# One core, spectral filter beside a shift-mixing MLP: the second group's statistics and transposes among the first group's products, and step one's pairs, unscalings and maxima in other places

## The chip, the core and the metric

The kernel runs on one core of a Trainium2 chip. The core has TensorE (matmuls and transposes by matmul), VectorE, ScalarE, GpSimd and SyncE, which here issues every DMA. Each engine works off its own instructions in the order in which the program lists them, and waits on semaphores for the others. In the profile TensorE is PE (and PEld for its weight loads), VectorE is DVE, ScalarE ACT, GpSimd POOL and SyncE SP. The metric is the device time of one execution in microseconds; the median of several runs counts.

## What is computed

`x` has 2048 tokens of 448 values. Two branches start from it and are summed with it:

```python
def _A_ref(x, w_r, w_i):                       # spectral filter
    X = rfft2(x); X = X * (w_r + 1j * w_i)
    return irfft2(X, (S, D))

def _B_ref(x, w1, w2, w3, w4):
    h = gelu(layernorm(x) @ w1)
    # the four quarters of h are shifted by +1, -1, +2, -2 tokens
    x1 = x + concat([g0, g1, g2, g3]) @ w2
    return x1 + gelu(layernorm(x1) @ w3) @ w4

xn = layernorm(x)
return x + _A_ref(xn, A_w_r, A_w_i) + _B_ref(xn, B_w1, B_w2, B_w3, B_w4)
```

w1 and w2 are 448 x 448, w3 is 448 x 1792, w4 1792 x 448; the filter has 2048 x 225 complex weights.

## The kernel before, in words

**Tiles.** Sixteen blocks of 128 tokens in four groups (`GRP`): group 0 is blocks 14, 15, 0, 1, group 1 is blocks 2 to 5, and so on. Precision comes from pairs of float16 numbers: a value is split into a high half (a copy by ScalarE) and a low half (the remainder, by VectorE, or GpSimd for some weights), and a product of two such values is three matmuls. A scale that keeps a weight in float16's range is worked out on the chip: for w1, ScalarE sums squares (line 252), VectorE adds them up (line 257), a small matmul with ones spreads the sum over the partitions (line 259), and VectorE makes powers of two of it (lines 261 to 266, `powers`). `split_w` (lines 272 to 280) then splits the weight.

**The start.** TensorE has nothing to do until the first loads land; `warm_up` gives it 24 matmuls on zeros. `norm1(g)` takes mean and variance of a group's four blocks (`bn_stats` and `bn_aggr`, lines 303 and 304), a first guess of the inverse root and an applied normalisation (lines 330 and 333, shared by GpSimd, VectorE and ScalarE), and hands back `refine`, ten small GpSimd instructions. `T1(g)` transposes the group, 16 matmuls into four PSUM banks (line 384), and evacuates each bank in a high half (line 388, ScalarE) and a low half (line 389, VectorE). Then come the products with w1 (line 415): 11 matmuls for each of the group's four units, 44 in all. For group 0 they come in two parts: the first two slices of all four units, 24 matmuls, and then the last two slices, 5 for each unit. After the 44, the sum matmul for w2 and group 1's transposes follow. `w1_unit` evacuates a unit by gelu and a split (lines 455 to 459); block transposes on SyncE and the products with w2 (line 474) finish the mixing.

**The MLP.** `ln2` normalises again (statistics, line 303; high half on ScalarE, line 504; low half on VectorE, lines 505 and 507; a block transpose on SyncE, line 509). `mlp` runs over groups of 256 tokens, `G`, and pairs of slices of w3, `fp`: `front` is 22 matmuls with w3 (line 395), a gelu (line 724) and a split into `hf` (lines 726 and 727); `back` is 12 matmuls with w4 (line 806), two fronts behind.

**Step one of the transform** runs beside the MLP's groups 1 and 2. `do_fold` loads two blocks of x, scales them on ScalarE (line 536) and folds them on GpSimd (lines 542 to 545); `step1_in` splits them (lines 552 and 553); `step1` is 12 matmuls for a block (line 562) into one of two banks, evacuated on ScalarE and VectorE into `y` (lines 566 and 567). Pairs of blocks are placed by the table `PACE` behind the last w4 matmul of a given `(G, fp)`. On VectorE beside it are seven unscalings of the residual (line 515, with loads into one buffer of two halves) and eight maxima over the filter's weights (line 270, with loads into another buffer of two halves); both are placed behind a front's split by `EARLY` and `WMAX`. The same two buffers serve `ln2` before. The maxima end in a scale (`w_scale_end`) that the transform's next step needs. After that come the transform's other steps and the rest of the MLP.

**Order.** A planner lists each engine's instructions by a simulated time and by priority, which goes by the order of the text apart from `prio`; `behind(key)` keeps what it encloses behind an instruction noted in `after`, on the same engine only. So a pin on VectorE doesn't hold the load that the pinned instruction needs.

Of the kernel before, what the change touches and what calls it, by code (L numbers as in the profile page):

```python
# [27 lines left out]
FIRST = 2  # L28
WARM = 24
ZPRE = 2.0 ** -7  # L30
# [94 lines left out]
def body(tc, nc, x, wf, w1, w2, w3, w4, c_g, c_n, c_small, out):  # L125
# [128 lines left out]
    def powers(m, n, key, tag="acc", spare=0):  # L254

        t = pc.tile([128, 2], F32, name=f"pt{key}")
        V.tensor_reduce(out=t[:, 0:1], in_=m[:, :n], axis=AX.X, op=ALU.add)
        pm = bank(tag, f"pm{key}") if isinstance(tag, str) else tag
        i = T.matmul(pm[:, 0:1], ones, t[:, 0:1], start=True, stop=True)
        after["p" + key] = (i.ins,)  # L260
        V.tensor_scalar(out=t[:, 1:2], in0=pm[:, 0:1], scalar1=2.0 ** -58, scalar2=None, op0=ALU.max)
# [3 lines left out]
        V.tensor_scalar(out=e[:, 1:2], in0=e[:, 0:1], scalar1=-1, scalar2=185 - spare << 23, op0=ALU.mult, op1=ALU.add)  # L265
        V.tensor_scalar(out=e[:, 2:3], in0=e[:, 0:1], scalar1=1, scalar2=69 + spare << 23, op0=ALU.mult, op1=ALU.add)
        return e.bitcast(F32)[:, 1:2], e.bitcast(F32)[:, 2:3]
# [4 lines left out]
    def split_w(hi, lo, src, s, low=None):  # L272
        if low is P:
            P.tensor_scalar(out=src, in0=src, scalar1=s, scalar2=0.0, op0=ALU.mult, op1=ALU.add)
# [3 lines left out]
        i = A.activation(out=hi, in_=src, func=AF.Copy, scale=s)  # L278
        j = V.scalar_tensor_tensor(out=lo, in0=src, scalar=s, in1=hi, op0=ALU.mult, op1=ALU.subtract)
        return i.ins, j.ins  # L280
# [16 lines left out]

    def stats(src, key, mv=None):
        if mv is None:
            mv = pc.tile([128, 4, 2], F32, tag="mv", bufs=3, name=f"mv{key}")  # L300
        for i, s in enumerate(src):
            st = pc.tile([128, 6], F32, tag="st", bufs=4, name=f"st{key}_{i}")
            V.bn_stats(out=st, in_=s)
            V.bn_aggr(out=mv[:, i, :], in_=st)
        return mv
# [4 lines left out]

    def norm1(g, apply):

        bs = GRP[g]
        n, b0 = len(bs), bs[0]
        mv = pc.tile([128, 4, 2], F32, name=f"mva{b0}")
        stats([xb(b) for b in bs], f"a{b0}", mv)
        a = pc.tile([128, 2 * n], F32, name=f"va{b0}")
# [58 lines left out]

    def transpose_split(srcs, dst, key, ts=range(4), at=0, tags=("tr",) * 4):
        c = slice(128 * at, 128 * at + 128 * len(srcs))
        for t in ts:
            pt = bank(tags[t], f"pt{key}{t}")  # L380
            w = 128 if t < 3 else 64
            with behind("T", key) if ("T", key) in after else contextlib.nullcontext():
                for i, s in enumerate(srcs):
                    m = T.transpose(pt[:w, 128 * i:128 * i + 128], s[:, 128 * t:128 * t + w], ident)
# [3 lines left out]
            i = A.activation(out=dst[:w, t, c], in_=pt, func=AF.Copy)  # L388
            j = V.tensor_tensor(out=lo, in0=pt, in1=dst[:w, t, c], op=ALU.subtract)  # L389
            after[key, t] = after[key] = i.ins, j.ins  # L390
# [86 lines left out]

    def ln2(bs, engines):

# [21 lines left out]
        for i in range(n):  # L501
            b, h, x_ = b0 + i, y[i // 2][:, i % 2], o[i // 2][:, i % 2]
            k = r[:, i:i + 1]
            u = A.activation(out=h[:, 0:D], in_=x_, func=AF.Copy, scale=k)
# [51 lines left out]
    def step1(b):  # L556
        t = xh_buf[b % 4]
        pm = bank("sp", f"ps1_{b}")
        for q in range(4):
            for n, (xi, ri) in enumerate(PASS):  # L560
                o = xi * 452 + 113 * q
                T.matmul(pm[:, 128 * q:128 * q + 128], t[:, o:o + 128], cR[ri][:, 128 * (q % 2):128 * (q % 2) + 128],  # L562
                         start=n == 0, stop=n == 2)
# [3 lines left out]
        V.tensor_tensor(out=y[1], in0=src, in1=y[0], op=ALU.subtract)  # L567

    sc = pc.tile([128, 4], F32, name="sc")

    def w_scale():
        wm = pc.tile([128, 8], F32, name="wm")
        t = stage("wl", 8 * DF, 1)
        for c in range(8):
            h = t[:, 4 * DF * (c % 2):4 * DF * (c % 2) + 4 * DF]
            SY.dma_start(h, wf.rearrange("c (p r) n -> (c p) (r n)", r=8)[:, 4 * DF * c:4 * DF * (c + 1)])
            with behind("f", *WMAX[c]):
                absmax(wm[:, c:c + 1], h)
        return wm

    def w_scale_end(wm):
        t = pc.tile([128, 4], F32, name="wt")
# [262 lines left out]

    def T1(g, ts=range(4)):
        if g not in xTs:
            xTs[g] = p1.tile([128, 7, 512], F16, tag="xT", bufs=2, name=f"xT{g}")
        transpose_split([xb(b) for b in GRP[g]], xTs[g], f"a{g}", ts,
                        tags=("mm", "mm", "tr", "tr") if g == 2 else ("tr", "tr", "acc", "acc"))  # L850

# [135 lines left out]
    for b in range(12, 16):  # L987
        w2_tile(b)
    ln2(range(12, 16), [P, A, P, A])
    close("p1")  # L990
# [8 lines left out]
    for i in range(4):  # L999
        P.memset(xh_buf[i][:, 904:], 0.0)  # L1000
    loads = stage("loads", 1808, 0)
    EARLY = {(1, 0): 1, (1, 1): 2, (1, 3): 3, (1, 5): 4, (1, 6): 5, (2, 1): 6, (2, 2): 7,
             (2, 3): "4", (2, 4): "5", (2, 5): "0"}

    def between(G, fp):
        if (G, fp) in EARLY:
            k, n = EARLY[G, fp], list(EARLY).index((G, fp))
            part = loads[:, 896 * (n % 2):896 * (n % 2) + 896]
            go = w4_sums(int(k), part) if isinstance(k, str) else unscale(k, part)
            with behind("f", G, fp):  # L1010
                go()

    mlp([1, 2], hook=between, ahead=AH, tags=("mm", "tr"))
    for b in range(0, NB, 2):
# [78 lines left out]
```

## Time and profile before

| | us |
|---|---|
| median of three runs | 412.37 |
| lowest and highest of the runs | 412.36, 414.42 |
| the profiled execution, whole | 414.05 |
| its span, first to last instruction | 412.2 |
| TensorE busy in the span | 401.3 |
| VectorE, ScalarE, GpSimd busy | 333.9, 255.8, 100.9 |

The profiled execution's mean granted TensorE clock is 0.996 of full speed. The profile's rows give a start and a duration, the engine, the line, the operation, what it writes and reads, shapes and a count of merged instructions; in square brackets stands how long the engine sat idle before, and whose end released it. Rows that start with a line number are groups: after the bar come busy microseconds and the mean of one in nanoseconds, after the next bar the idle time ahead of them.

### The profile page before, as it was taken

To read this page: it belongs to the slowest core of one execution; us is meant where nothing else is said; L and a number is where in the kernel's file an instruction comes from. 1 tells how busy PE (TensorE), PEld (TensorE's weight loads), DVE (VectorE), ACT (ScalarE), POOL (GpSimd) and SP (SyncE) were. 2 spreads that over 40 slices of the span, in tenths; PEclk is the share of its full clock that TensorE was granted. 3 is DMA by queue.
4 is the path that set the end of the run, shared out by engine and by line. 5 is a ranking of instruction groups with operands and counts; after the bars stand their busy time and mean duration, and the time that the engine had idled before them with its cause. 6 is when DMAs were issued, how large, how long until landed. Compare 5 with 4: busy or idle time off the path is not lost.

```text
span 412.2 us, 8724 instructions
## 1 busy us (share of the span) xinstructions
PE 401.3 (97%) x3389; PEld 298.0 (72%) x3389; DVE 333.9 (81%) x702; ACT 255.8 (62%) x434; POOL 100.9 (24%) x173
## 2 busy tenths in 40 slices
PE   6999999999999999999999999999999999999996
PEld 2655545755658677777787888877777779998995
DVE  5878998999775858987798888956799998966645
ACT  4679789982567857565498888954453453553331
POOL 7688520110035866420011221110000000000000
PEclk9899999999999999999999999999999999999999
DMA  8976985479297557435355556610021012100101
GB/s 272 377 278 128 245 170 146 81 122 198 54 238 208 173 173 233 139 131 143 84 147 152 147 142 161 163 32 14 0 91 68 25 67 82 56 23 0 46 2 45
DMA packets 54596, 52.07 MB, mean 126 GB/s; under 512 B 35678, under 2 KB 48542, under 8 KB 54556
## 3 DMA queue, kind: packets, MB, share of 16 engines
q1 hardware_dynamic: 54556, 51.53, 46.0%
q8 instruction: 26, 0.43, 0.4%
q14 instruction: 14, 0.11, 0.1%
HBM read 38.28 MB, written 3.67 MB: 102 GB/s over the span
## 4 chain that ended last, share of the span: by engine, by line
PE 60%; DMA 2%; issue 1%; DVE 1%; POOL 0%; SPq 0%
PE pw L395 24%; PE acc L806 16%; PE side L776 4%; PE acc L776 3%; PE pu L665 3%; PE pe L686 2%; PE pp L620 2%; PE px L637 2%; PE py L707 2%; DMA wl<-wf 2%; PE ps L562 1%; DVE wm L270 0%; POOL xr L543 0%; POOL f L545 0%; DVE y L567 0%
## 5 line engine op out<-in xcount | busy, mean ns | idle before, releaser
L395 PE MATMUL pw<-x2mem,w3p 128*128 128x256 f16 x1232 | 150.6, 273 | 0.0
L395 PEld LDWEIGHTS <-w3p 128*128 128x128 f16 x1232 | 119.3, 98 | 19.9
L806 PE MATMUL acc<-w4p,hf 128*128 128x448 f16 (+1 forms) x516 | 105.6, 348 | 0.7 <-ACT hf L726 0.7
L806 PEld LDWEIGHTS <-hf 128*128 128x128 f16 x516 | 49.6, 98 | 37.6 <-ACT hf L726 1.0
L724 ACT ACTIVATE pw<-pw,pe 128x512 f32<-128x512 f32 x42 | 27.4, 653 | 29.4 <-PE pw L395 29.4
L727 DVE SCALAR_TENSOR_TENSOR hf<-pw,h,hf 128x512 f16<-128x512 f32 x42 | 31.3, 745 | 12.8 <-ACT hf L726 12.7
L415 PE MATMUL pw<-w1p,xT 128*128 128x448 f16 x176 | 35.5, 356 | 1.1 <-DVE xT L389 0.6
L474 PE MATMUL pw<-w2p,h 128*128 128x448 f16 x176 | 35.6, 353 | 0.9 <-DMA h<-x2mem 0.8
L646 POOL TENSOR_TENSOR z<-te 128x450 f32<-128x450 f32 x16 | 15.7, 982 | 70.3 <-DVE te L644 70.3
L415 PEld LDWEIGHTS <-xT 128*128 128x128 f16 x176 | 17.2, 99 | 18.3 <-ACT xT L388 1.2
L726 ACT ACTIVATE hf<-pw,h 128x512 f16<-128x512 f32 x42 | 28.8, 686 | 1.8 <-PE acc L806 0.8
L474 PEld LDWEIGHTS <-h 128*128 128x128 f16 x176 | 16.9, 98 | 17.1 <-DMA h<-x2mem 2.3
L742 ACT ACTIVATE hz<-g,h 128x896 f16<-128x896 f32 x14 | 14.6, 1042 | 22.6 <-DVE g L739 22.5
L776 PEld LDWEIGHTS <-hz 128*128 128x128 f16 x294 | 28.2, 98 | 0.4
L627 ACT ACTIVATE pf<-pp 64x450 f16<-64x450 f32 x32 | 17.4, 543 | 12.4 <-DVE pf L628 8.0
L628 DVE TENSOR_TENSOR pf<-pp,pf 64x450 f16<-64x450 f32 x32 | 19.9, 622 | 3.4 <-ACT pf L627 3.0
L743 DVE SCALAR_TENSOR_TENSOR hz<-g,h,hz 128x896 f16<-128x896 f32 x14 | 16.1, 1149 | 7.6 <-ACT hz L742 7.6
L553 DVE TENSOR_TENSOR xh<-f,xh 128x452 f16<-128x452 f32 x16 | 12.4, 809 | 7.4 <-ACT xh L552 7.4
L642 ACT ACTIVATE te<-px 64x450 f32<-64x450 f32 x32 | 17.3, 541 | 1.2 <-DMA wc<-wf 0.5
L545 POOL TENSOR_TENSOR f<-xr 128x452 f32<-128x452 f32 x16 | 17.5, 1116 | 0.6
L736 ACT ACTIVATE g<-pw,pe 128x512 f32<-128x512 f32 x14 | 9.5, 681 | 10.1 <-PE pw L395 10.0
L690 ACT ACTIVATE e<-pe 128x226 f32<-128x226 f32 x16 | 5.8, 360 | 16.0 <-DVE vh L700 9.0
(188 smaller groups left out, 716.5 us busy)
## 6 DMA issues: line engine op xcount, KB each, us to landing
wc<-wf SPq DMA_DIRECT2D x32, 225.0 KB, 3.6
wl<-wf SPq DMA_DIRECT2D x8, 450.0 KB, 4.2
xt<-x SPq DMA_DIRECT2D x8, 448.0 KB, 7.4
xf<-x SPq DMA_DIRECT2D x8, 448.0 KB, 3.7
loads<-x SPq DMA_DIRECT2D x7, 448.0 KB, 4.2
out<-xt SPq DMA_DIRECT2D x13, 224.0 KB, 1.9
w3raw<-w SPq DMA_DIRECT2D x3, 896.0 KB, 11.1
gn<-c_g SPq DMA_DIRECT2D x16, 128.0 KB, 3.1
```

What stands on the lines that cost most here:

```text
L395: T.matmul(ps_out, wp[:, wi + t, cols], xT[:, xi + t, tok], start=t == 0 and wi + xi == 0, stop=t == 3 and wi == 4)
L415: T.matmul(pm[:, :D], xTs[g][:, xi + t, 128 * i:128 * i + 128], w1p[:, wi + t], start=t == 0 and p == 0, stop=t == 3 and p == 2)
L474: T.matmul(pm[:, :D], h[:, k], w2p[:, w], start=n == 0, stop=n == 10)
L545: P.tensor_tensor(out=f[:, :, k:k + 2].rearrange("p b s d -> p s b d"), in0=u[:, :, 0], in1=u[:, :, 1], op=op)
L627: A.activation(out=hi, in_=src, func=AF.Copy)
L628: V.tensor_tensor(out=lo, in0=src, in1=hi, op=ALU.subtract)
L642: A.activation(out=e[64 * h:64 * h + 64], in_=px_[64 - 64 * h:128 - 64 * h, :2 * DF], func=AF.Copy)
L724: A.activation(out=pm, in_=pm, func=AF.Gelu_apprx_tanh, scale=r3)
L726: i = A.activation(out=h[:, 0], in_=pm, func=AF.Copy, scale=h3)
L727: j = V.scalar_tensor_tensor(out=h[:, 1], in0=pm, scalar=h3, in1=h[:, 0], op0=ALU.mult, op1=ALU.subtract)
L776: m = T.matmul(to, h[:, hi, 128 * blk:128 * blk + 128], b[wi], start=new and n == 0, stop=n == 2 and (last if blk in (2, 5, 3, 0) else end ...
L806: m = T.matmul(to, h[:, hi, o:o + 128], w4p[0][:, wi, f, r], start=first and f % 2 == 0 and n == 0, stop=end and f % 2 == 1 and n == 2, sk ...
```

## The change

In the start: 26 warm-ups in place of 24. Group 0's first four transposes come ahead of the w1 sum matmul, their high half is copied at once, and their low half is kept until the scale's arithmetic is done. Group 1's four `bn_stats` are pinned one by one: behind group 0's normalisation, behind the sum, and behind the first and second low halves. The refinement of group 0 goes behind GpSimd's scaling of w1's last slice. After the first unit's 5 late products all of group 1's transposes come, and the other three units' 15 products are pinned behind these.

In `ln2` of the last four blocks, the high halves on ScalarE are pinned behind the split of the last front of group 0.

In step one: the first five pairs come one `(G, fp)` later. Of the unscalings, two stay behind fronts, and five are pinned behind a pair's evacuations, as all the maxima are: by pair, `AFTER` and `WMAX` list them. The three w4 sums stay where they were; the end of the scale comes one place earlier.

```diff
-WARM = 24
+WARM = 26
-PACE = [(1, 0), (1, 1), (1, 2), (1, 4), (1, 5), (2, 0), (2, 1), (2, 3)]
+PACE = [(1, 1), (1, 2), (1, 3), (1, 5), (1, 6), (2, 0), (2, 1), (2, 3)]
-WMAX = [(1, 4), (1, 5), (1, 6), (2, 0), (2, 1), (2, 2), (2, 3), (2, 4)]
+WMAX = [[0], [1], [2], [3, 4], [5], [6], [7], []]
+AFTER = [[], [3], [4], [5], [6], [7], [], []]
...
     def stats(src, key, mv=None, pins=None):
...
-            V.bn_stats(out=st, in_=s)
+            with behind(*pins[i]) if pins else contextlib.nullcontext():
+                V.bn_stats(out=st, in_=s)
...
             i = A.activation(out=dst[:w, t, c], in_=pt, func=AF.Copy)
-            j = V.tensor_tensor(out=lo, in0=pt, in1=dst[:w, t, c], op=ALU.subtract)
+            todo.append((key, t, i, lo, pt, dst[:w, t, c]))
+        if late is None:
+            low()
...
-            u = A.activation(out=h[:, 0:D], in_=x_, func=AF.Copy, scale=k)
+            with behind(*late) if late else contextlib.nullcontext():
+                u = A.activation(out=h[:, 0:D], in_=x_, func=AF.Copy, scale=k)
...
     n1 = [norm1(0, [P, V, A, V])]
+    T1(0, range(1), True)
     with behind("n", 0):
         s1, r1 = powers(m1, 4, "1", "mm")
     first = [bank("mm" if k < 2 else "sp", f"pw1_0{k}") for k in range(4)]
+    with behind("e1"):
+        low()
     for t in range(4):
-        with behind("p1"):
-            T1(0, [t])
+        if t >= 1:
+            with behind("p1"):
+                T1(0, [t])
...
-    for unit in enumerate(first):
+    n = 1
+    for unit in list(enumerate(first))[:n]:
         w1_in(0, [unit], [2, 3])
-    with behind("w1", 3):
+    with behind("ps"):
         n1[0][0]()
-    with behind("w1", 1):
-        n1.append(norm1(1, [P, V, A, V]))
+    n1.append(norm1(1, [P, V, A, V], [("n", 0), ("r1",), ("a0", 0), ("a0", 1)]))
     with behind("w1", 3):
         squares(m2, flat(w2s))
-    T1(1, range(3))
+    T1(1)
+    with behind("T", "a1"):
+        for unit in list(enumerate(first))[n:]:
+            w1_in(0, [unit], [2, 3])
     with behind("n", 1):
         s2, r2 = powers(m2, 1, "2", first[0][:, 448:512])
-    with behind("p2"):
-        T1(1, [3])
...
-    ln2(range(12, 16), [P, A, P, A])
+    ln2(range(12, 16), [P, A, P, A], ("f", 0, 6))
...
-        if (G, fp) in EARLY:
...
+        if (G, fp) in ((1, 0), (1, 1)):
+            go = unscale(fp + 1, half(fp))
             with behind("f", G, fp):
                 go()
...
         with behind("m", *PACE[b // 2]):
             step1(b)
             step1(b + 1)
-    with behind("X", 14):
-        wm = w_scale()
+        with behind("y", b + 1):
+            for p in AFTER[b // 2]:
+                unscale(p, half(p + 1))()
+            for c in WMAX[b // 2]:
+                w_scale(wl, c)
+    for n, j in enumerate((4, 5, 0)):
+        go = w4_sums(j, half(n))
+        with behind("f", 2, 3 + n):
+            go()
     close("pfd")
-    with behind("m", 2, 4):
-        w_scale_end(wm)
+    with behind("m", 2, 3):
+        w_scale_end()
```

More of the change, by code (lines that the diff above doesn't have):

```diff
@@ L256, in powers @@
         t = pc.tile([128, 2], F32, name=f"pt{key}")
-        V.tensor_reduce(out=t[:, 0:1], in_=m[:, :n], axis=AX.X, op=ALU.add)
+        after["r" + key] = (V.tensor_reduce(out=t[:, 0:1], in_=m[:, :n], axis=AX.X, op=ALU.add).ins,)
         pm = bank(tag, f"pm{key}") if isinstance(tag, str) else tag
@@ L273, in split_w @@
         if low is P:
-            P.tensor_scalar(out=src, in0=src, scalar1=s, scalar2=0.0, op0=ALU.mult, op1=ALU.add)
+            after["ps"] = (P.tensor_scalar(out=src, in0=src, scalar1=s, scalar2=0.0, op0=ALU.mult, op1=ALU.add).ins,)
             i = A.activation(out=hi, in_=src, func=AF.Copy)
@@ L375, in behind, with transpose_split @@
             yield
-    def transpose_split(srcs, dst, key, ts=range(4), at=0, tags=("tr",) * 4):
+    def transpose_split(srcs, dst, key, ts=range(4), at=0, tags=("tr",) * 4, late=None):
         c = slice(128 * at, 128 * at + 128 * len(srcs))
@@ L476, in w2_tile, with ln2 @@
                                op0=ALU.mult, op1=ALU.add)
-    def ln2(bs, engines):
+    def ln2(bs, engines, late=None):
         n, b0 = len(bs), bs[0]
@@ L566, in step1, with w_scale, w_scale_end @@
         A.activation(out=y[0], in_=src, func=AF.Copy)
-        V.tensor_tensor(out=y[1], in0=src, in1=y[0], op=ALU.subtract)
+        after["y", b] = (V.tensor_tensor(out=y[1], in0=src, in1=y[0], op=ALU.subtract).ins,)
     sc = pc.tile([128, 4], F32, name="sc")
[L571 to L581, printed above, removed]
+    def w_scale(t, c):
+        h = t[:, 4 * DF * (c % 2):4 * DF * (c % 2) + 4 * DF]
+        SY.dma_start(h, wf.rearrange("c (p r) n -> (c p) (r n)", r=8)[:, 4 * DF * c:4 * DF * (c + 1)])
+        absmax(wm[:, c:c + 1], h)
+    wm = pc.tile([128, 8], F32, name="wm")
+    def w_scale_end():
         t = pc.tile([128, 4], F32, name="wt")
@@ L844, in body, with T1 @@
     flat = lambda t: t.rearrange("p a n -> p (a n)")
-    def T1(g, ts=range(4)):
+    def T1(g, ts=range(4), late=None):
         if g not in xTs:
@@ L849, in T1 @@
         transpose_split([xb(b) for b in GRP[g]], xTs[g], f"a{g}", ts,
-                        tags=("mm", "mm", "tr", "tr") if g == 2 else ("tr", "tr", "acc", "acc"))
+                        tags=("mm", "mm", "tr", "tr") if g == 2 else ("tr", "tr", "acc", "acc"), late=late)
     def turn(g):
@@ L1001, in body, with half @@
     loads = stage("loads", 1808, 0)
-    EARLY = {(1, 0): 1, (1, 1): 2, (1, 3): 3, (1, 5): 4, (1, 6): 5, (2, 1): 6, (2, 2): 7,
-             (2, 3): "4", (2, 4): "5", (2, 5): "0"}
+    def half(n):
+        return loads[:, 896 * (n % 2):896 * (n % 2) + 896]
     def between(G, fp):
-        if (G, fp) in EARLY:
-            k, n = EARLY[G, fp], list(EARLY).index((G, fp))
-            part = loads[:, 896 * (n % 2):896 * (n % 2) + 896]
-            go = w4_sums(int(k), part) if isinstance(k, str) else unscale(k, part)
+        if (G, fp) in ((1, 0), (1, 1)):
+            go = unscale(fp + 1, half(fp))
             with behind("f", G, fp):
@@ L1013, in body @@
     mlp([1, 2], hook=between, ahead=AH, tags=("mm", "tr"))
+    wl = stage("wl", 8 * DF, 1)
     for b in range(0, NB, 2):
```

14 lines of the change are left out of this document (10 added, 4 removed).

## The prediction, made before the changed kernel ran

> **What bounds the kernel now.** I read the page first: how much of the span each engine works.
>
> ```profile
> span 412.2 us, 8724 instructions
> PE 401.3 (97%) x3389; PEld 298.0 (72%) x3389; DVE 333.9 (81%) x702; ACT 255.8 (62%) x434; POOL 100.9 (24%) x173
> ```
>
> TensorE is busy for all but 10.9 us, so a change that leaves its work alone can gain only idle time, or time at a lower clock. The view of waits, TensorE's rows, names the idle time (microseconds, times, longest):
>
> ```profile
> PE pm L259 <- DVE pt L257: 2.2, 1, 2.2
> PE ps L562 <- DVE y L567: 1.4, 2, 0.9
> PE pw L474 <- DMA h<-x2mem: 0.8, 3, 0.4
> PE acc L806 <- ACT hf L726: 0.7, 1, 0.7
> PE pw L415 <- DVE xT L389: 0.6, 2, 0.3
> PE pw L415 <- DMA xT<-x: 0.4, 1, 0.4
> ```
>
> Then the start in stretches (length, busy time of each engine, granted clock, DMA share, GB/s):
>
> ```profile
> core 0: us, PE busy (x) PEld busy (x) DVE busy (x) ACT busy (x) POOL busy (x), PEclk, DMA share, GB/s
> 4.10:7.51 3.41, 3.41 (x17) 1.57 (x16) 3.00 (x11) 1.09 (x3) 3.00 (x2) 1.00 1.04 352
> 7.51:10.93 3.42, 1.21 (x10) 0.74 (x8) 2.07 (x8) 2.13 (x7) 1.14 (x2) 1.00 1.02 322
> 10.93:14.34 3.41, 3.41 (x17) 2.75 (x16) 2.96 (x9) 3.22 (x7) 1.25 (x2) 0.50 1.06 334
> ```
>
> After a stretch in which TensorE worked 1.21 of 3.42 us (35%), the clock stood at 0.50 for 3.41 us. Half of that, 1.7 us, is work lost. The profiled execution took 414.05 us (1.85 outside its span); the runs shown took 412.36, 412.37 and 414.42, with a median of 412.37. The difference of 1.68 is about the price of that stretch, so I take the median run to be one without it. That is inferred: only the profiled execution has a clock record.
>
> **The start, part by part.** TensorE's timeline is the scale:
>
> ```profile
> 10.19 0.38 PE L259 MATMUL pm<-pt,ones 128*128 128x1 f32 x2 [2.21 <-DVE pt L257]
> 10.44 3.21 PE L384 MATMUL pta<-ident,xt 128*128 128x128 f32 x16
> 22.21 0.28 PE L259 MATMUL pw<-pt,ones 128*128 128x1 f32 x2
> 22.35 1.94 PE L384 MATMUL pta<-ident,xt 128*128 128x128 f32 x16
> 24.62 1.14 PE L415 MATMUL pw<-w1p,xT 128*128 128x448 f16 x3 [0.32 <-DVE xT L389]
> 26.05 8.11 PE L415 MATMUL pw<-w1p,xT 128*128 128x448 f16 x41 [0.29 <-DVE xT L389]
> ```
>
> The first row's idle time is the hole in which the fillers go. At full clock a transpose costs 1.94 / 16 = 0.12 us and a product 8.11 / 41 = 0.198. The second group's products end at 34.16; that is the point I compare.
>
> *Warm-ups and first transposes.* Two more warm-ups cost 3.41 / 17 = 0.20 each and lie in the 2.21 us of idle, so they cost nothing; without that cover, 0.4. Four transposes (0.48) go ahead of the sum matmul, into the same hole: the last share of the first group's normalisation ends at 8.64 + 0.75 = 9.4 (row of line 330 below), the sum matmul starts at 10.19. The idle time, from 7.98 on, falls apart into about 1.0 and 0.3, and the stretch 7.51 to 10.93 holds 1.21 + 0.4 + 0.48 = 2.1 us of work, 61%. The share at which the clock falls lies somewhere between 35%, which brought it down, and 100%, which didn't. I take 61% to be on the safe side: half of a stretch seems the simplest border, but no row gives it. The trace alone bounds what this is worth from 0 to 1.7 us.
>
> The Trainium skill (TensorE: Matmul & The Clock Gate, Why this matters for your kernels) tells one to avoid idle gaps over about 3 us between matmul bursts; by it a gap of 2.2 us would be harmless and the fillers worth nothing. The trace differs: 2.21 us were followed by 0.50.
>
> *Statistics into gaps of VectorE.* Rows of VectorE, ScalarE and GpSimd, and the landing of the second group's first load (issued at 3.66):
>
> ```profile
> xt<-x SPq DMA_DIRECT2D x1, 448.0 KB, 5.8
> 8.64 0.75 ACT L330 ACTIVATE xt<-xt,nma,vy 128x448 f32<-128x448 f32 x1
> 9.98 0.16 DVE L257 TENSOR_REDUCE pt<-m 128x1 f32<-128x4 f32 x1 [0.73 <-ACT xr L252]
> 10.61 0.16 DVE L261 TENSOR_SCALAR pt<-pm 128x1 f32<-128x1 f32 x1 [0.47 <-PE pm L259]
> 10.99 0.15 DVE L265 TENSOR_SCALAR pe<-pe 128x1 int32<-128x1 int32 x1
> 11.62 0.66 ACT L278 ACTIVATE w1p<-w1s,pe 128x448 f16<-128x448 f32 x1
> L303 DVE BATCH_NORM_STATS2 sta<-xt 128x6 f32<-128x448 f32 x4 | 2.2, 605 | 0.0
> L389 DVE TENSOR_TENSOR xT<-pta,xT 128x512 f16<-128x512 f32 x3 | 2.0, 678 | 0.4 <-ACT xT L388 0.4
> L279 DVE SCALAR_TENSOR_TENSOR w1p<-w1s,pe,w1p 128x448 f16<-128x448 f32 x2 | 1.3, 672 | 0.0
> 17.68 0.38 DVE L304 BATCH_NORM_AGGREGATE mva<-sta 128x2 f32<-128x6 f32 x4
> 19.03 0.94 DVE L333 TENSOR_SCALAR xt<-xt,vy,nma 128x448 f32<-128x448 f32 x2
> 20.33 0.71 POOL L333 TENSOR_SCALAR xt<-xt,vy,nma 128x448 f32<-128x448 f32 x1
> ```
>
> VectorE idles 0.73 and 0.47 us around the sum. The first two statistics (0.55 to 0.6 each) go there. The data land at 3.66 + 5.8 = 9.5, so the first statistic runs 9.5 to 10.1, and the second sits ahead of line 261: both together delay the scale by about 0.25, to 11.39. This is a cost, since the split of w1, and with it the first product, waits for it. Against it, the first evacuation on ScalarE, which stood ahead of line 278, is done before the scale is known, so the first w1 half ends at 11.39 + 0.66 = 12.05 in place of 12.28. Bounds for the first product: 11.8 with no delay, 12.4 with a whole statistic (0.6) in the way; I take 12.1. The evacuations' second halves, pinned behind the scale's arithmetic, keep VectorE from holding that up.
>
> VectorE then works without a break from about 11.45: four evacuations (2.7), two w1 halves (1.3), two statistics (1.1), to 16.55; averages and scalars take 1.35 (17.68 to 19.03), then 0.94 for applying them. The second group is normalised at 18.85 instead of 21.04. GpSimd's refinement, moved behind its second scaling, no longer stands in front of its share.
>
> *Transposes among the products.* 29 products run first: 12.1 + 0.2 (the second w1 half) + 29 x 0.198 = 18.05. The transposes are pinned there and wait until 18.85: 0.8 us in which 15 ready products stand behind them. Then 1.94, 15 x 0.198 = 2.97 (covering the evacuations that cost two waits before), 0.28 and 44 x 0.198 = 8.7 end at 32.75. Against 34.16 that is **-1.4 us**. Bounds: without waits 31.75 (-2.4); with normalisation as late as before, 21.04 + 1.94 + 2.97 + 0.28 + 8.7 = 34.95 (+0.8).
>
> **The pin behind the last front of group 0.**
>
> ```profile
> 116.64 2.33 ACT L504 ACTIVATE y<-y,vs 128x448 f16<-128x448 f32 x4
> 119.54 0.69 ACT L726 ACTIVATE hf<-pw,h 128x512 f16<-128x512 f32 x1
> 120.29 2.48 PE L806 MATMUL acc<-w4p,hf 128*128 128x448 f16 x12 [0.69 <-ACT hf L726]
> ```
>
> Without the four activations ahead of it, hf would be there 2.3 us sooner: **-0.7**, the whole gap. What is late next: their halves on VectorE, their transposes on SyncE, then the loads into the same buffer, and ScalarE's scaling for the first fold, all by about 2.3 us. The first pair's place is one step later too, which covers the fold. Bounds 0 and -0.7.
>
> **Step one, unscaling and maxima.**
>
> ```profile
> 135.85 2.39 DVE L553 TENSOR_TENSOR xh<-f,xh 128x452 f16<-128x452 f32 x2 [1.04 <-ACT xh L552]
> 138.90 0.83 PE L562 MATMUL ps<-csm,xh 128*128 128x128 f16 x12 [0.85 <-DVE y L567]
> 159.91 1.09 DVE L270 TENSOR_REDUCE wm<-wl 128x1 f32<-128x900 f32 x1 [1.28 <-DMA wl<-wf]
> 160.92 1.28 DVE L567 TENSOR_TENSOR y<-ps,y 128x512 f16<-128x512 f32 x2
> SPq L576 <- DVE wm L270: 6.6, 6, 2.4
> 161.65 1.50 PE L562 MATMUL ps<-csm,xh 128*128 128x128 f16 x24 [0.56 <-DVE y L567]
> L515 DVE SCALAR_TENSOR_TENSOR xt<-xt,s,loads 128x896 f32<-128x896 f32 x7 | 9.3, 1334 | 0.0
> ```
>
> Nothing is added: eight maxima and five of the seven unscalings move, each with its load on SyncE. There a maximum's load waits until the maximum two before it has left their shared buffer (the row of line 576), and loads for folds stand behind it on the queue; three fold buffers cover a few us of that. The 0.56 has a maximum waiting 1.28 us for its load with the evacuation behind it; pinned behind the evacuation, this order can't recur. The 0.85 comes from a late fold; the pair comes one front and one back (34 matmuls) later, which is more than the 2.3 by which its fold is late; so it should shrink, if not go. I take **-1.1** of the 1.41; bounds 0 and -1.4, or a loss (below).
>
> **Sum.** 414.05 - 1.4 - 0.7 - 1.1 = **410.85 us**, which is 1.5 under the median of the runs shown, since that run, by my reading, already lacks the slow stretch: against it the start gives nothing (34.16 - 1.7 = 32.46, I expect 32.75).
>
> **Rivals.**
> *Pinned transposes wait for a late normalisation* (slower). A statistic placed ahead of line 261 or of the w1 halves on VectorE delays everything behind it; if the second group comes only at 21.04, TensorE waits 3.0 us beside 15 ready products: 414.05 + 0.8 - 0.7 - 1.1 = 413.05. It decides from about 20.4 on. For it: VectorE has no gap left between 11.4 and 19. Against: the sum above leaves 2.2 us to that.
> *The clock falls all the same.* If transposes count for little at the gate, the stretch holds 1.21 + 0.4 = 47%, nearer to the 35% that closed it. The half-clock stretch costs 1.7, of which 0.8 fills the wait for the transposes: 411.75. For it: nothing separates the two yet; against it: the stretch at 0.50 was largely transposes and the clock rose at its end. The Trainium skill (same page, Part 4: PE-mode transpose) says that transposes don't count as busy in the same way; the row 10.93:14.34 speaks rather against it.
> *Step one only moves its waits*: a load into a shared buffer lands late, VectorE stops on an unscaling or maximum, and hf, xh and y stand behind it. Pair three has two maxima and an unscaling, 2 x 1.09 + 1.33 = 3.5 us of VectorE. Without the gains of this stage 411.95; with one stall of 1.3 in the rows' size, 413.25.
> *More closes*: no wait at 18 us, and the waits on h and xT (1.2) shrink: 414.05 - 2.4 - 0.7 - 1.4 = 409.55, down to 408.35.
>
> **Chances.** Forecast 0.36, late normalisation 0.15, clock 0.14, step one 0.15, more closes 0.20. The range leaves out the ends of the first and last: 409.0 to 413.3; the likeliest case alone has 409.9 to 411.7. About 0.5%, 2.06 us, is what a measurement of this kernel can tell from no change: faster means under 410.31, slower over 414.43. Faster: nearly all of the last case and under half of the forecast, 0.35. Slower needs two of the losses at once: 0.11. The rest, 0.54, lies between.
>
> **What would show it.** Clock 1.00 through the stretch after 10.9; first product near 12.1; second group's transposes starting near 18.9 with products on both sides; their evacuations leaving no gap; no wait of line 806 near 120; no wait of line 562. I am wrong if the transposes start after 20.4, if the clock shows 0.50, if line 515 or 270 shows waits on loads over 1 us with TensorE idle behind them, or if gaps of that sum open between 35 and 115 us, where ScalarE and VectorE are nearly full.

## The result, and the profile after

The changed kernel takes 410.88 us (median of ten runs, 410.37 to 411.44), the kernel before 412.37 (ten runs, 411.89 to 414.42). The ratio is 0.9954, with a 95% interval of 0.9940 to 0.9968. The predicted time was 410.85. The profiled execution of the changed kernel took 410.88 us as well, so its trace is that of a typical run.

The page of the changed kernel, first its span and busy times:

```profile
span 409.1 us, 8749 instructions
PE 400.4 (98%) x3391; PEld 297.5 (73%) x3391; DVE 336.9 (82%) x702; ACT 256.1 (63%) x434; POOL 103.2 (25%) x173
```

TensorE has two warm-ups more and otherwise the same work; 0.9 us of its busy time and 2.2 us of its idle time have gone (idle 10.9 before, 8.7 now). The view of waits of the same kernel, TensorE's rows (total, times, longest; the wait of the first warm-up is left out):

```profile
PE pw L486 <- DMA h<-x2mem: 1.2, 2, 0.7
PE pw L260 <- DVE pt L258: 0.7, 1, 0.7
PE pm L260 <- DVE pt L258: 0.5, 1, 0.5
PE pta L387 <- POOL xt L336: 0.5, 1, 0.5
PE pw L486 <- DMA w2p<-w2p: 0.4, 1, 0.4
PE pw L427 <- ACT w1p L280: 0.4, 1, 0.4
PE pw L427 <- DVE w1p L281: 0.3, 1, 0.3
```

The rows of step one (1.4) and of the last front of group 0 (0.7) have no successor: this list holds nothing later than 40 us. Lines have moved: 260 is the sum matmul (259 before), 387 the transposes (384), 427 the w1 products (415), 486 the w2 products (474).

To see where the 3.1 us of span (412.2 to 409.1) come from, I cut both traces at the last matmul of the sixth front of group 0. The view of stretches, columns as in the prediction; first the kernel before, then the changed one:

```profile
0.00:109.20 109.20, 103.73 (x599) 60.14 (x600) 92.60 (x266) 80.94 (x136) 46.39 (x120) 0.98 0.75 190
109.20:412.20 303.00, 297.59 (x2792) 237.83 (x2790) 241.32 (x437) 174.90 (x298) 54.54 (x53) 1.00 0.36 103
```

```profile
0.00:108.70 108.70, 103.31 (x601) 59.68 (x602) 97.49 (x274) 81.39 (x136) 47.89 (x120) 1.00 0.78 196
108.70:409.10 300.40, 297.11 (x2792) 237.81 (x2790) 239.44 (x429) 174.74 (x298) 55.35 (x53) 1.00 0.36 103
```

Behind the cut TensorE has the same 2792 matmuls in both, so the two parts can be compared. Between these two executions the start gave 0.5 us and the rest 2.6. The sum of the prediction had 1.4 and 1.8. Its total came out almost exactly; its parts did not.

The start on TensorE, changed kernel (the timeline; idle time and releaser in brackets):

```profile
10.32 0.38 PE L260 MATMUL pm<-pt,ones 128*128 128x1 f32 x2 [0.50 <-DVE pt L258]
...
12.44 1.67 PE L427 MATMUL pw<-w1p,xT 128*128 128x448 f16 x8 [0.37 <-ACT w1p L280]
14.46 4.13 PE L427 MATMUL pw<-w1p,xT 128*128 128x448 f16 x21 [0.34 <-DVE w1p L281]
19.34 0.38 PE L260 MATMUL pw<-pt,ones 128*128 128x1 f32 x2 [0.75 <-DVE pt L258]
20.18 1.97 PE L387 MATMUL pta<-ident,xt 128*128 128x128 f32 x16 [0.46 <-POOL xt L336]
21.98 11.32 PE L427 MATMUL pw<-w1p,xT 128*128 128x448 f16 x59
```

The transposes start at 20.18, where 18.85 was forecast, and the second group's products end at 21.98 + 11.32 = 33.30, where 32.75 was. But the 59 products run in one piece: no evacuation leaves a gap, as forecast. What the transposes waited for stands on VectorE and GpSimd (the same view):

```profile
16.79 1.03 DVE L325 TENSOR_SCALAR vy<-va 128x8 int32<-128x8 int32 x1
...
18.06 0.18 DVE L328 SCALAR_TENSOR_TENSOR nma<-mva,vy 128x4 f32<-128x4 f32 x1
18.28 0.93 DVE L336 TENSOR_SCALAR xt<-xt,vy,nma 128x448 f32<-128x448 f32 x2
19.13 0.15 DVE L258 TENSOR_REDUCE pt<-m 128x1 f32<-128x1 f32 x1
...
16.76 1.03 POOL L278 TENSOR_TENSOR w1p<-w1s,w1p 128x448 f16<-128x448 f32 x1
18.32 0.20 POOL L358 TENSOR_TENSOR vw<-vr,vy 128x4 f32<-128x4 f32 x1
...
19.42 0.71 POOL L336 TENSOR_SCALAR xt<-xt,vy,nma 128x448 f32<-128x448 f32 x1
```

The scale for the normalisation is ready at 18.24 (18.06 + 0.18), and VectorE applies its shares at once, until 19.21. GpSimd starts its share only at 19.42 and ends at 20.13. The refinement of group 0 (lines 345 to 354 here) ends at 18.35; between then and 19.42 GpSimd works off other small instructions, which the planner put ahead: three that follow the refinement (lines 358 to 360) and the first of the second group's own refinement (line 345, between the first two). They cost the transposes 0.5 to 1.0 us: without them these could have started at 19.21 at the earliest or, with the sum matmul of w2 ahead of them as here, at 19.72. The other delay is VectorE's: its scalar of line 325, 128 x 8 elements, took 1.03 us beside a GpSimd subtraction that began 0.03 earlier and ended with it. And the sum matmul of w2, which the forecast had behind the transposes, runs ahead of them at 19.34, as soon as VectorE's line 258 lets it.

### The profile page after: what moved, and what is told of

Read it like the earlier page. It is cut to its first block, busy times and chain, and to the rows that moved or that the text cites. A ratio compares the mean times of both kernels' runs of the same rounds, so it can differ in the third digit from the quotient of the medians.

```text
span 409.1 us, 8749 instructions
## 1 busy us (share of the span) xinstructions
PE 400.4 (98%) x3391; PEld 297.5 (73%) x3391; DVE 336.9 (82%) x702; ACT 256.1 (63%) x434; POOL 103.2 (25%) x173
## 4 chain that ended last, share of the span: by engine, by line
PE 86%; DVE 5%; DMA 3%; POOL 2%; ACT 1%; SPq 1%; issue 1%
PE pw L407 33%; PE acc L816 23%; PE pw L486 6%; PE side L786 4%; PE acc L786 3%; PE pu L675 3%; PE ps L575 3%; PE pe L696 2%; PE pp L630 2%; PE px L647 2%; PE py L717 2%; PE pw L427 2%; DMA xt<-x 1%; DVE sta L306 1%; DVE xT L401 1%; DMA w2p<-w2p 1%
## 5 line engine op out<-in xcount | busy, mean ns | idle before, releaser
L816 PE MATMUL acc<-w4p,hf 128*128 128x448 f16 (+1 forms) x516 | 104.2, 348 | 0.0
L737 DVE SCALAR_TENSOR_TENSOR hf<-pw,h,hf 128x512 f16<-128x512 f32 x42 | 31.3, 745 | 12.7 <-ACT hf L736 12.4
L558 POOL TENSOR_TENSOR f<-xr 128x452 f32<-128x452 f32 x16 | 19.7, 1250 | 0.6
L566 DVE TENSOR_TENSOR xh<-f,xh 128x452 f16<-128x452 f32 x16 | 14.3, 916 | 4.9 <-ACT xh L565 4.9
L555 POOL TENSOR_TENSOR xr<-xf 128x452 f32<-128x452 f32 x8 | 9.2, 1154 | 24.4 <-issue 17.6
```

The costliest lines, as they stand in the source:

```text
L558: P.tensor_tensor(out=f[:, :, k:k + 2].rearrange("p b s d -> p s b d"), in0=u[:, :, 0], in1=u[:, :, 1], op=op)
L737: j = V.scalar_tensor_tensor(out=h[:, 1], in0=pm, scalar=h3, in1=h[:, 0], op0=ALU.mult, op1=ALU.subtract)
L816: m = T.matmul(to, h[:, hi, o:o + 128], w4p[0][:, wi, f, r], start=first and f % 2 == 0 and n == 0, stop=end and f % 2 == 1 and n == 2, sk ...
```

## The experiments

Twelve kernels ran, in three groups, each on one chip beside new runs of the kernel before (412.64, 412.55 and 412.38 us there). Their expectations were written before they ran.

### The kernel before once more

No edit.

> The kernel before, unchanged, for the clock record of each of its runs. Theory (the half-clock stretch after 10.9 us makes its long runs long): the runs with a mean clock of 0.996 take 1.2 to 2 us more than those at 0.999 or above, which lie near 412.0. Rival (the spread has another cause): long and short runs show the same mean clock.

412.53 us, ratio 0.9997 (0.9984 to 1.0009). What it adds is clock records of many runs. Of the 70 runs of this kernel in the three groups, 18 had a mean granted clock of 0.995 or 0.996, and 52 one of 0.999 or 1.000. The first take 413.42 us on average, the others 412.39. So the median run has no stretch at half clock, as the prediction inferred, and runs with one take 1.0 us more, not 1.7 (nor the 1.2 to 2 of the expectation). The rest of the distance between the profiled execution (414.05) and the median is in the part behind the cut: 303.0 us there, 302.1 in this experiment's trace, where TensorE's waits near 120, 139 and 161 us sum to 1.3 in place of 2.1. The same program can thus have 0.8 us more or less of the waits that the change is meant to remove.

### The start alone

```diff
-WARM = 24
+WARM = 26
...
     n1 = [norm1(0, [P, V, A, V])]
+    T1(0, range(1), True)
...
-        n1.append(norm1(1, [P, V, A, V]))
+    n1.append(norm1(1, [P, V, A, V], [("n", 0), ("r1",), ("a0", 0), ("a0", 1)]))
...
-    T1(1, range(3))
+    T1(1)
+    with behind("T", "a1"):
+        for unit in list(enumerate(first))[n:]:
+            w1_in(0, [unit], [2, 3])
```

> The start's part of the change alone. Theory A (against a run of before without the half-clock stretch the start gives nothing; it only takes that stretch away): median 412.0 to 412.5, runs within 1.2 us of each other, mean clock 0.999 or more in all. Rival B (the start is worth its 0.9 us at the second group's end against every run): median 411.3 to 411.6. Rival C (what it gains is lost to waits on block transposes between 35 and 60 us and more): over 412.6.

411.17 us, ratio 0.9959 (0.9945 to 0.9974): better than any number expected. The gain isn't in the start. In this trace the part up to the sixth front takes 108.9 us, and the rest 300.3, with no wait of TensorE in it, though step one's code is that of before. The planner lists every engine's instructions anew when anything changes, and from the changed start it lists step one in another order, in which no load makes TensorE wait. Its maxima start at 150.82, 155.27 and 158.71, each ahead of TensorE's need, where before had one at 159.91 with TensorE waiting behind it.

### Step one and the pin

PACE, WMAX, AFTER, the unscalings and maxima behind `y`, and the pin in `ln2`; the start is that of before.

```diff
...
-    ln2(range(12, 16), [P, A, P, A])
+    ln2(range(12, 16), [P, A, P, A], ("f", 0, 6))
...
+        with behind("y", b + 1):
+            for p in AFTER[b // 2]:
+                unscale(p, half(p + 1))()
+            for c in WMAX[b // 2]:
+                w_scale(wl, c)
```

> Step one's part and the pin behind group 0's last front, with the start of before. Theory (the gaps near 120, 139 and 161 us, 2.1 us in all, go to the end whole): median 410.2 to 410.6, with the spread of before, some runs at 0.996 mean clock and 1.2 to 2 us longer. Rival (part of it comes back as other waits, and the rest of the measured gain is the start's): 411.0 to 411.8.

410.33 us, ratio 0.9947 (0.9927 to 0.9967). The four runs at full clock have a mean of 410.16, so this half of the change is worth 412.39 - 410.16 = 2.2 us by itself, as its theory had it, and the whole change (410.88) looks slower than this half.

### The pin alone

```diff
-    ln2(range(12, 16), [P, A, P, A])
+    ln2(range(12, 16), [P, A, P, A], ("f", 0, 6))
```

> The pin alone: in the second layer norm of the last four blocks the high halves stand behind the split of group 0's last front. Theory: the wait of the w4 product near 120 us (0.69) goes and nothing else changes: median 411.6 to 411.8. Rival (without the later places of step one's pairs the delayed fold makes the first pair late): 412.3 or more, with a wait of line 562 or of a w4 product between 128 and 140 us.

412.69 us, ratio 1.0001 (0.9984 to 1.0019): nothing that the runs can tell, where the prediction had put 0.7. (Six of the twelve runs have the lower clock; the other six average 412.27, those of the kernel before on the same chip 412.44.) The wait near 120 is gone, as forecast, and so is the one near 139, but the one near 161 is larger. The rival had the time right and the place of the wait wrong. The timeline of this kernel:

```profile
161.28 1.50 PE L563 MATMUL ps<-csm,xh 128*128 128x128 f16 x24 [1.77 <-DVE y L568]
```

and its chain of waits (start, length, what):

```profile
148.56 1.07 POOL xr L544
...
150.07 4.38 DMA wl<-wf
...
155.59 3.92 DMA wl<-wf
160.54 0.69 DVE y L568
```

The same chain in the kernel before:

```profile
148.57 1.07 POOL xr L543
...
150.08 4.45 DMA wl<-wf
...
155.67 4.22 DMA wl<-wf
160.92 0.69 DVE y L567
```

GpSimd's fold, SyncE's issue (between the first two rows), a load of the filter's weights, a maximum (between the two loads) and the next load into the same half stand at the same instants, to 0.08 us, up to the start of the second load; the evacuation comes 0.38 earlier, as that load is shorter. TensorE comes earlier, and waits there instead: the three waits sum to 0.69 + 0.85 + 0.56 = 2.1 before and to 1.8 here. The chain isn't tied to an instant: in the trace with 26 warm-ups alone, where all that comes ahead of it is earlier, GpSimd's piece of it starts at 146.82. But the pin doesn't move it. A wait that is removed ahead of a chain that stays gives nothing; the chain has to be moved as well.

### Step one without the pin

The third experiment without its change to `ln2`.

```diff
-            with behind(*late) if late else contextlib.nullcontext():
-                u = A.activation(out=h[:, 0:D], in_=x_, func=AF.Copy, scale=k)
+            u = A.activation(out=h[:, 0:D], in_=x_, func=AF.Copy, scale=k)
```

> Step one's part without the pin and without the start's part. Theory (each wait removed goes to the end, since the chain of folds, loads and maxima no longer holds a fixed time at 160 us): 0.3 to 0.7 over the 410.2 that step one's part and the pin gave at full clock, 410.5 to 410.9, with a wait of the w4 product near 120 us. Rival (the pin is of no use there either, as when it stood alone): 410.0 to 410.3.

412.78 us, ratio 1.0013 (1.0001 to 1.0025), beyond both ranges expected. Step one's edits alone give nothing either. The timeline of this kernel:

```profile
118.88 2.47 PE L804 MATMUL acc<-w4p,hf 128*128 128x448 f16 x12 [0.43 <-ACT hf L724]
139.27 2.39 DVE L554 TENSOR_TENSOR xh<-f,xh 128x452 f16<-128x452 f32 x2 [0.37 <-ACT xh L553]
...
142.41 0.77 PE L563 MATMUL ps<-csm,xh 128*128 128x128 f16 x11 [1.10 <-DVE y L568]
```

and that of the third experiment, with the pin, at the same place:

```profile
138.34 1.29 DVE L569 TENSOR_TENSOR y<-ps,y 128x512 f16<-128x512 f32 x2 [0.47 <-ACT y L568]
140.54 2.43 DVE L555 TENSOR_TENSOR xh<-f,xh 128x452 f16<-128x452 f32 x2
```

Without the pin the scalings of `ln2` stand ahead of `hf` on ScalarE again and leave their wait at 118.88 (0.43, where the kernel before had 0.69 and, in its second trace, 0.30), and the planner lists a pair's split of 2.39 us between the pair's two evacuations, so that the next pair waits 1.10 us for a bank. With the pin both evacuations stand together and the split behind them. The two parts, each worth nothing alone, are worth some 2.2 us together.

### 26 warm-ups alone

```diff
-WARM = 24
+WARM = 26
```

> The kernel before with 26 warm-ups and nothing else. Theory (the clock falls where less than about half of a 3.41 us stretch is work): the fillers bring the worst stretch from 35% to 47%, so fewer runs show the mean clock of 0.996 or less than the 11 of 36 of the kernel before, though not none; the undisturbed ones stay at 412.2 to 412.6. Rival 1 (the border lies below 47%): no run under 0.999. Rival 2 (only a whole stretch's idle time counts): as many low clocks as before.

411.90 us, ratio 0.9986 (0.9975 to 0.9997). One of 12 runs has the lower clock, against 18 of 70 with 24 warm-ups. The eleven others average 411.89, under the 412.2 to 412.6 expected and under the 412.43 of the kernel before at full clock on the same chip; every engine has the same order as before, the two warm-ups aside, and where these 0.5 us come from is not shown. In stretches, then for the transposes alone (there TensorE, its weight loads, clock):

```profile
7.33:10.74 3.41, 1.75 (x12) 1.02 (x11) 2.23 (x9) 2.15 (x7) 1.14 (x2) 1.00 1.01 316
10.74:14.16 3.42, 3.42 (x25) 2.33 (x23) 2.99 (x9) 3.26 (x7) 1.28 (x3) 1.00 1.06 323
...
7.33:10.74 3.41, 0.51 (x5) 0.62 (x6) 1.00 1.01 316
```

1.75 of 3.41 us were enough to keep the clock. (Where the clock doesn't change at a stretch's edges, these are counted back in steps of 3.413 us, the length of a half-clock stretch in the traces' clock records, from the change that the trace has at the end, when TensorE has nothing left to do.) This trace is also the kernel before's start at full clock: its second group's products are

```profile
24.38 8.11 PE L415 MATMUL pw<-w1p,xT 128*128 128x448 f16 x41 [0.31 <-DVE xT L389]
```

and end at 32.49, which is the prediction's 32.46 for such a start. (The trace of step one without the pin, with 24 warm-ups and at full clock too, has 24.70 + 8.11 = 32.81.)

### Step one, the pin and 30 warm-ups

The third experiment with `WARM = 30`.

> Step one's part and the pin, with the start of before but 30 warm-ups, which fill the hole ahead of the w1 sum to about 0.9 us. Theory (of the start's part only the clock is of use, and fillers do that alone): all runs at a mean clock of 0.999 or more, median 410.0 to 410.3, under the whole change's 410.9. Rival (the fillers run late in some executions and hold up the sum, or the start's part is of use otherwise): 410.6 or more.

410.30 us, ratio 0.9943 (0.9928 to 0.9957), none of six runs at the lower clock. With the clock kept by warm-ups alone, the old start and the new step one are 0.4 to 0.6 us faster than the whole change (410.88 before the experiments, 410.73 below). That compares different chips, and the intervals overlap (0.9943 to 0.9969 below); the profiled executions differ by 0.2 us, 408.9 and 409.1. So a loss by the new start is likely but small.

### The changed kernel once more, and with 24 warm-ups

```diff
-WARM = 26
+WARM = 24
```

> The changed kernel, unchanged, beside the next three on the same chip. Theory (at full clock the start's part costs 0.7 us where step one's waits are already gone): 410.7 to 411.1, no run under a mean clock of 0.999. Rival (the chip made the difference to the kernel with step one's part alone): 410.1 to 410.4.

> The changed kernel with 24 warm-ups, so that of the fillers only the four early transposes are left. Theory (transposes count as work at the clock gate: 1.21 + 0.48 of 3.42 us in the worst stretch, 49%, as with two more warm-ups): at most one run in ten under 0.999, median as with 26. Rival (they don't count, so the worst stretch stays near 35%): about three runs in ten at 0.996 and some 1 us longer, as before the change.

410.73 us (ratio 0.9956, 0.9943 to 0.9969) and 410.90 (0.9958, 0.9946 to 0.9971). With 24 warm-ups two of six runs have the lower clock, but they took 410.94 and 411.05 and are hardly longer than the others. The theory's one in ten fails, and so does the rival's 1 us. The profile is of one of these two; its stretches, the last row for the transposes alone:

```profile
8.07:11.48 3.41, 2.08 (x15) 1.45 (x15) 3.15 (x12) 2.59 (x8) 1.12 (x2) 1.00 1.04 319
11.48:14.90 3.42, 3.42 (x14) 1.86 (x13) 3.42 (x10) 3.42 (x8) 2.76 (x8) 0.50 1.06 332
...
8.07:11.48 3.41, 1.65 (x12) 1.31 (x13) 1.00 1.04 319
```

and a row of its timeline:

```profile
20.29 1.97 PE L387 MATMUL pta<-ident,xt 128*128 128x128 f32 x16 [0.46 <-POOL xt L336]
```

The transposes start at 20.29, 0.1 later than in the changed kernel's trace, although 3.42 us were at half clock: the slow products fill the time in which TensorE waits for the normalisation anyway. And the clock fell after a stretch with 2.08 us of work, 61%.

### More products ahead of the transposes

One number in the changed kernel: how many units have their 5 late products ahead of the second group's transposes.

```diff
-    n = 1
+    n = 2
```

and 3, and 4 (all).

> The changed kernel with two units' late products ahead of the second group's transposes in place of one. Theory (TensorE's waits of 0.75 and 0.46 us ahead of these transposes are the start's loss, and five products, 1.0 us, fill them): median 409.9 to 410.2, and these two waits at 0.3 us or less together. Rival (what TensorE gains there it waits for block transposes of h between 35 and 60 us): 410.6 to 411.0, with waits of line 486 grown by as much.

> The changed kernel with three units' late products ahead of the second group's transposes. With two, TensorE still waited 0.74 us for GpSimd's share of the normalisation. Theory (five more products, 1.0 us, fill that): 409.2 to 409.5. Rival (from here on the waits on h and on the evacuations behind the transposes take over, with five products left as their cover): 409.7 to 410.4.

> The changed kernel with all four units' products ahead of the second group's transposes, as before the change; early statistics and first transposes stay. Theory (the pin of the transposes among the products costs more wait than its cover of the evacuations saves): no wait ahead of the transposes, waits of 0.5 to 0.8 us after them, median 410.2 to 410.6. Rival (the early statistics hold up the first products, 0.37 and 0.34 us, and that is the loss): 410.8 to 411.2.

| units ahead | us | ratio to before, interval |
|---|---|---|
| 1, the change | 410.73 (410.88) | 0.9956, 0.9943 to 0.9969 |
| 2 | 409.62 | 0.9928, 0.9913 to 0.9943 |
| 3 | 410.36 | 0.9945, 0.9932 to 0.9957 |
| 4 | 410.53 | 0.9949, 0.9935 to 0.9963 |

Two units are best, and faster than both kernels: 2.8 us under the kernel before (409.62 and 412.37) and 1.3 under the change. Two and four ran on one chip, one and three on another; no run with two is as slow as the fastest of the others. The time with two is better than its theory had it, with three as its rival, with four as its theory. The timeline with two units:

```profile
20.43 1.97 PE L387 MATMUL pta<-ident,xt 128*128 128x128 f32 x16 [0.74 <-POOL xt L336]
22.24 10.42 PE L427 MATMUL pw<-w1p,xT 128*128 128x448 f16 x54
...
16.89 0.18 DVE L325 TENSOR_SCALAR vy<-va 128x8 int32<-128x8 int32 x1
17.31 0.88 DVE L328 SCALAR_TENSOR_TENSOR nma<-mva,vy 128x4 f32<-128x4 f32 x1
...
17.13 1.04 POOL L278 TENSOR_TENSOR w1p<-w1s,w1p 128x448 f16<-128x448 f32 x1
```

Five more products, 1.0 us, run ahead of the transposes. The waits there fall from 1.2 to 0.74 us, not to the 0.3 expected, since GpSimd's share comes late here too; the products end at 32.66 in place of 33.30. The other half of the gain lies behind: TensorE's waits from 33 us on, 1.6 with one unit, are 0.9 here. With three units the transposes don't wait for the normalisation any more, but too few products are left behind them to cover the evacuations:

```profile
23.42 0.83 PE L427 MATMUL pw<-w1p,xT 128*128 128x448 f16 x3 [0.30 <-DVE xT L401]
24.73 8.11 PE L427 MATMUL pw<-w1p,xT 128*128 128x448 f16 x41 [0.48 <-DVE xT L401]
```

These products end at 32.84, 0.2 later than with two; the rest of the 0.7 between the two medians is not located.

## Why the prediction came out

The time was right by luck: two errors of opposite sign cancelled. Counted against a run at full clock, the prediction had +0.3 for the start and -1.8 for the pin and step one, -1.5 in all. The runs show about +0.6 for the start (410.73 to 410.88 with it, 410.16 to 410.34 without it at full clock) and about -2.1 for the rest (412.39 to the same), -1.5 in all. The parts don't add up in any order, though: the start alone gave -1.2 (411.17), and beside it the pin and step one add only -0.3.

**The clock.** Right in kind: the median run is one without the half-clock stretch, and 26 warm-ups keep the clock in nearly all runs (11 of 12 with nothing else changed). The price was mis-sized, 1.0 for 1.7: half of the stretch was counted as lost work, without asking what waits shrink behind it (from 33 to 110 us on TensorE they are 1.2 in the traces of the kernel before, both with the stretch, and 1.8 with 26 warm-ups and without it), and the difference between the profiled execution and the median, which seemed to confirm it, holds later waits too.

**61% on the safe side.** The step that failed here is "half of a stretch seems the simplest border". A stretch with 61% of work let the clock fall (2.08 us, of which 1.65 transposes), and one with 51% kept it (1.75, of which 0.51 transposes). The changed kernel kept it at 2.54, with 2.17 of transposes:

```profile
9.13:12.54 3.41, 2.54 (x20) 2.10 (x20) 3.12 (x13) 2.53 (x7) 0.94 (x2) 1.00 1.06 319
...
9.13:12.54 3.41, 2.17 (x16) 1.77 (x16) 1.00 1.06 319
```

No one share separates these three. Suppose that the gate, whatever it is that grants the clock, weighs a transpose's time by one factor w. Then the three ask for 0.43 + 1.65 w to be less than both 1.24 + 0.51 w and 0.37 + 2.17 w, which holds for w from 0.12 to 0.71. The stretch of the kernel before that lost the clock has 1.21 us of work, of which 0.49 are transposes:

```profile
7.51:10.93 3.42, 0.49 (x5) 0.60 (x6) 1.00 1.02 322
```

It asks for 0.72 + 0.49 w to be less than 0.37 + 2.17 w, so w is over 0.21. By this, transposes count, but for less than warm-ups and products do. The Trainium skill (TensorE: Matmul & The Clock Gate, Part 4: PE-mode transpose) says that transposes don't count as busy in the same way. The prediction held that the row 10.93:14.34 spoke rather against it; the measured rows agree with the page, except that transposes cannot count for nothing: without them this stretch has 0.37 us of work, and the clock stayed. This is worked out from few stretches, the upper bound from a single one, and neither w nor the form with one factor was measured by itself.

**First product at 12.1.** 12.44, at the upper bound given (12.4). All of the start shifts from one execution to the next: in the profile of the repeated run the sum matmul comes at 9.99 in place of 10.32, and the first product at 12.11.

**Second group normalised at 18.85.** It was at 20.13. The step that failed: "GpSimd's refinement, moved behind its second scaling, no longer stands in front of its share." The refinement itself ended at 18.35, within 0.1 us of the time when the share could start; but GpSimd's list had four more small instructions ahead of the share, until 19.42, which the prediction did not count. On VectorE the shares ended at 19.21, 0.36 late, and line 325 alone took 0.85 more than its 0.18. The wait behind the pin was 0.75 + 0.46 = 1.2 for 0.8 (the first part for the sum matmul of w2, which stood ahead), with the first product's two waits (0.37 and 0.34) before it. The rival of a late normalisation, which was to decide from 20.4 on, came within 0.2 us of its point.

**Waits behind the start.** Not forecast: from 33 us on the waits on h and w2 sum to 1.2 + 0.4, where the kernel before had 0.8 on h and 0.4 on xT.

**The pin, -0.7 whole, and step one, -1.1.** Their sum was mis-sized and their division wrong. All waits went (2.1 in the one execution that the prediction read, 1.3 in the other), but neither part removes anything alone. "The whole gap" took the wait of line 806 as if what lies behind it moved along; the chain of the kernel before, 148.57 to 160.92, has GpSimd, SyncE and two transfers in it and isn't moved by a TensorE that is 0.7 earlier. It was to be read in the chain of waits, which the prediction did not use for this sum. The rival that step one only moves its waits describes what each part does alone.

**Behind the cut.** The length of the parts ahead of it and behind it in each profiled execution, and TensorE's waits behind it:

| kernel | ahead | behind | waits |
|---|---|---|---|
| before | 109.2 | 303.0 | 2.1 |
| before once more | 109.2 | 302.1 | 1.3 |
| 26 warm-ups alone | 107.9 | 302.1 | 1.3 |
| pin alone | 109.3 | 302.5 | 1.8 |
| step one without the pin | 108.1 | 302.5 | 1.5 |
| start alone | 108.9 | 300.3 | none |
| step one, pin, 30 warm-ups | 108.5 | 300.4 | none |
| the change | 108.7 | 300.4 | none |
| two units ahead | 107.8 | 300.4 | none |

The part behind the cut has two kinds of lengths: 300.3 to 300.4 without waits, 302.1 to 303.0 with them. The edits of step one together with the pin are one way to the first kind, and the new start happens to be another. It is the planner's order that makes the difference, and not an earlier start: with 26 warm-ups alone the part ahead is 1.3 us shorter, every engine's order is that of before, and the waits stay; with the new start VectorE's order in step one is another, and they are gone. Which of the planner's rules does it in the start alone was not tried.

## What to carry to other kernels

Cut the trace of both kernels at an instruction that they share, with the same count of matmuls behind it, before crediting a gain to a part: a right total can hide two wrong terms. A wait ahead of a chain of other engines and transfers can be worth nothing until the chain is moved too; read the chain of waits, not the sum of waits. Where a pinned piece must wait, count what every engine still has ahead of its share, and put a little more ready work in front of the pin, but leave enough behind it to cover the evacuations.

## What was unexpected of the hardware

**VectorE held until a GpSimd instruction ended.** In the changed kernel line 325 took 1.03 us and line 328 0.18; with two units ahead line 325 took 0.18 and line 328 0.88. Each time it was the instruction that began just behind GpSimd's subtraction of line 278, and it ended within 0.03 us of it (17.82 and 17.79; 18.19 and 18.17). GpSimd's instruction kept its 1.03 to 1.04. The Trainium skill (SBUF — State Buffer, SBUF: two separate sides) tells of a port pair that the two engines share as an exclusive lock, kept for a whole instruction. The trace agrees, with 0.7 to 0.85 us more for an instruction of 0.18. Not every VectorE instruction is held: beside the subtraction before it, 15.36 to 16.40 in the changed kernel, lines 307 and 401 took 0.17 and 0.68, as they do elsewhere.

**The gate reacts to partly busy stretches.** Stretches of 3.41 us with 1.21 and with 2.08 us of work were followed by a clock of 0.50 for one such stretch, though no idle gap in them was as long as 2.3 us.

**The same kernel, two clocks.** 18 of 70 runs of the kernel before had the lower clock; two more warm-ups brought it to 1 of 12 (and six more gave 0 of 6 in the kernel with 30). What differs between executions can be seen in the warm-ups' pace. In the kernel before, 7 took 2.88 us up to 4.10, 0.41 each, and 17 took 3.41 in the next stretch, 0.20 each. In the trace of step one without the pin, whose start is the same, the slow pace lasts until 7.25 (9 warm-ups from 4.10 to 7.25, against 16):

```profile
5.46 4.07 PE L834 MATMUL wps<-wsrc 128*128 128x512 f16 x14
10.15 0.38 PE L260 MATMUL pm<-pt,ones 128*128 128x1 f32 x2 [0.62 <-DVE pt L258]
```

The same 24 warm-ups end at 9.53 there in place of 7.98, the hole ahead of the sum is 0.62 us in place of 2.21, and the clock stays at 1.00. The changed kernel's profiled execution is of that kind too (12 from 4.10 to 7.25), so its 26 warm-ups end at 9.21, where the prediction's sum has them end near 8.4. How well fillers cover a hole thus depends on when, in that execution, they stop being slow.
